# Attention with mixed heads and a mixture of experts: two pairs of heads of scores in one step, products with v and a third of the rows in the next, on the same banks

## The chip, the cores and the metric

One core of a Trainium2 chip runs the whole program. The metric is the device time of one execution in microseconds (us). PE is TensorE, DVE VectorE, ACT ScalarE, POOL GpSimd, and SP the engine whose queue issues most transfers.

## What is computed

```python
scores = (1/8) * q @ k.T                       # 8 batches, 12 heads, 448 x 448, 64 columns a head
scores = einsum('bhij,hg->bgij', scores, w_pre)
attn = softmax(scores)                         # over j
attn = einsum('bhij,hg->bgij', attn, w_post)
x = (attn @ v) as 3584 rows of 768
logits = x @ w_gate; e = argmax(logits); p = softmax(logits)[e]
out = p * (relu(x @ w1[e]) @ w2[e])            # one of 8 experts for each row
```

## The kernel before

**Attention.** Each batch of 448 queries is cut into four tiles T of 120, 120, 120 and 88 queries, 32 tiles in all. Heads go in pairs (6 pairs c or p). For a tile the scores of one pair (`qk`, L231: six matmuls, with q and k each split in a rounded high part and a remainder) go to the two banks `bank_s`, and ACT copies them to the tile's buffer `SI` (`evict_s`, L243). SP then issues transfers that turn a *block* of up to 20 queries so that (query, head) lies along the partitions (`relayout`, L251, tiles `sb`, four buffers). A tile of 120 queries has 6 blocks, one of 88 has 5, the last of them a single half. So a batch has 23 blocks and the program 184, and there is one *step* u for each.

In step u one block goes through each stage: `mix` (L258, PE, scores mixed over heads by w_pre, into `bank_m`), `maxima` (L271, DVE), `powers` (L278, ACT, exponentials and their sums). In step u+1 follow `recip` (L287, DVE) and `weigh` (L294, POOL), in step u+2 `post` (L303, PE, mixing by w_post, into `bank_p`) and `evict_p` (L319, DVE, into the tile's `PT`). `bank_m` and `bank_p` have one buffer each, so a step's mix follows the exponentials of the step before.

Beside that the steps carry work of other tiles. Before the change each step has `qk` and `evict_s` of one pair of the next tile, 8 to 3 steps ahead of its first block (QLEAD, L482), and `av` (L341, eight matmuls of one pair's PT with v) of the tile before, into `bank_a`, half of the pairs in each of its two banks. After three pairs `evict_x` (L350, DVE) copies the products out, `rows` (L361, PE, three matmuls with the identity and w_gate beside it) turns them into rows, `evict_r` (L367, ACT) copies the rows out and `logits` (L374, DVE) adds up the gate's part. When a tile's rows are complete, `store_x` (L382, SP) writes them to memory, `choose`, `rank`, `place`, `token` (L391 to L446) pick each row's expert and count, and `scatter` (L448, POOL) writes the row's number and weight into a table.

**The order** is written by hand. `at(u, stage, ...)` puts a call in step u (L485), ORDER (L549) gives the order of the stages within a step, and the loop at L578 emits them so; each engine keeps that order. `load_v` of the next batch (L147: 1152 KB and twice 192 KB) stands in a batch's step 9, after that step's `relayout` and `store_x`. For the first tile of a batch the scores of pair 0 come last in their step (stage "qk2").

**The end of attention.** The first expert's six tiles of w1 are loaded and split (`load_w`, L470: a transfer of 512 KB, a copy on ACT, a subtraction on DVE) one in each of the last steps from L586 on, load and split in the same step. All six `av` of the last tile stand at the end of its last step.

**The experts.** L592 on is the same in both kernels: each expert's rows are gathered through the table, transposed and multiplied, PE without a pause. The first gather needs the table and the rows of the last tile.

Of the kernel before, what the change touches and what calls it, by code (L numbers as in the profile page):

```python
# [42 lines left out]
def attn_moe_kernel(ctx, tc, qT, kT, v, w_pre, w_post, w_gate, w1, w2, out):  # L43
# [46 lines left out]
    bank_s = ps_s.tile([P, 2, 512], F32, name="bs")  # L90
    bank_a = ps_s.tile([P, 2, 512], F32, name="ba")
# [139 lines left out]
    def qk(T, c, bank):  # L231
        b, it, ni = geom[T][:3]
        if c == 0:
            SI[T] = si_p.tile([IT, H, S], F32, name="si")
        qh, ql = QQ[T]
        kh, kl = KK[b, c]
        for n, (qx, kx) in enumerate(((qh, kh), (qh, kl), (ql, kh))):
            for r in range(2):
                hs = slice(r * D, (r + 1) * D)
                nc.tensor.matmul(out=bank[:ni, r, :S], lhsT=qx[hs, c, :ni],  # L240
                                 rhs=kx[hs, :], start=(n == 0), stop=(n == 2))

    def evict_s(T, c, bank, copy):  # L243
        ni = geom[T][2]
        copy(out=SI[T][:ni, 2 * c:2 * c + 2, :], in_=bank[:ni, :, :S])  # L245
# [92 lines left out]
    def acc(g):  # L338
        return bank_a[:, g, :3 * IT].rearrange("p (c i) -> p c i", i=IT)

    def av(T, p):  # L341
        b, it, ni = geom[T][:3]
        for c in range(NJ):
            for r in range(2):
                h = 2 * p + r
                nc.tensor.matmul(out=acc(p // 3)[r * D:(r + 1) * D, p % 3, :ni],  # L346
                                 lhsT=VV[b][:, c, h * D:(h + 1) * D],
                                 rhs=PT[T][:, c, h, :ni], start=(c == 0), stop=(c == NJ - 1))

    def evict_x(T, g):  # L350
        ni = geom[T][2]
        if g == 0:
            XT[T] = x_p.tile([P, NPAIR, IT], F32, name="xt")
        nc.vector.tensor_copy(out=XT[T][:, 3 * g:3 * g + 3, :ni], in_=acc(g)[:, :, :ni])  # L354
# [3 lines left out]
    def rows_bank(part):  # L358
        return bank_a[:, part, :3 * XG].rearrange("p (c x) -> p c x", x=XG)

    def rows(T, part):  # L361
        ni = geom[T][2]
        for c in range(3):
            nc.tensor.matmul(out=rows_bank(part)[:ni, c, :], lhsT=XT[T][:, part * 3 + c, :ni],
                             rhs=xg[:, part * 3 + c, :], start=True, stop=True)

    def evict_r(T, part):  # L367
        ni = geom[T][2]
        if part == 0:
            XR[T] = x_p.tile([IT, NPAIR, P], F32, name="xr", bufs=1)  # L370
        nc.scalar.copy(out=XR[T][:ni, part * 3:part * 3 + 3, :],
                       in_=rows_bank(part)[:ni, :, :P])

    def logits(T, part):  # L374
        ni = geom[T][2]
        if part == 0:
            LG[T] = sm_p.tile([IT, 2, NE], F32, name="lg")
        nc.vector.reduce_sum(out=LG[T][:ni, part, :],
                             in_=rows_bank(part)[:ni, :, P:XG].rearrange("p c e -> p e c"),
                             axis=AX.X)  # L380
# [8 lines left out]
    RK = slice(496, 496 + NE), slice(496 + NE, 512)  # L389

    def choose(T):  # L391
        b, it, ni = geom[T][:3]
        lg2 = LG.pop(T)
        lg = sm_p.tile([IT, NE], F32, name="lgs")
        nc.vector.tensor_add(out=lg[:ni], in0=lg2[:ni, 0, :], in1=lg2[:ni, 1, :])
# [12 lines left out]

    def rank(T):
        ni = geom[T][2]  # L410
        ohb = DD[T][2]
        for lhs, m, cols in ((tri[:ni, :ni], ni, RK[0]), (ones[:ni, :], P, RK[1])):
            nc.tensor.matmul(out=bank_a[:m, 1, cols], lhsT=lhs, rhs=ohb[:ni], start=True, stop=True)
# [8 lines left out]
    def place(T):  # L422
# [3 lines left out]
        nc.vector.tensor_tensor(out=pos[:ni], in0=bank_a[:ni, 1, RK[0]], in1=state["base"][:ni],  # L426
# [3 lines left out]
        nc.vector.tensor_tensor(out=nbase, in0=bank_a[:, 1, RK[1]], in1=state["base"], op=ALU.add)  # L430
# [42 lines left out]


# [13 lines left out]
    vec, act = nc.vector.tensor_copy, nc.scalar.copy  # L488
    for u, (T, s) in enumerate(blocks):
        at(max(u - RLEAD, -1), "relayout", relayout, T, s)  # L490
        at(u, "mix", mix, T, s)
        at(u, "max", maxima, T, s)
        at(u, "exp", powers, T, s)
        at(u + 1, "recip", recip, T, s)
        at(u + 1, "weigh", weigh, T, s)
        at(u + PL, "post", post, T, s)
        at(u + PL, "evict_p", evict_p, T, s)
    for T in range(NTILE):
        b, it, ni = geom[T][:3]
        u0, n = ustart[T], len(geom[T][3])  # L500
        if T > 1:
            at(u0 - 12, "load", load_q, T)
            for part in range(2):
                at(u0 - 10 + part, "split", split_q, T, part)
        if T:
            for c in range(NPAIR):
                u = u0 - QLEAD + c
                if u < 0:
                    continue
                late = c == 0 and it == 0  # L510
                at(u, "qk2" if late else "qk", qk, T, c, bank_s)
                at(u, "evict_s2" if late else "evict_s", evict_s, T, c, bank_s, act)
        if it == 0 and b + 1 < B:
            U = ustart[T + 4]
            at(u0 + 9, "load", load_v, b + 1)
            for c, (ul, us) in enumerate(((15, 12), (14, 11), (10, 8), (9, 7), (7, 6), (6, 5))):
                at(U - ul, "load", load_k, b + 1, c)
                at(U - us, "split", split_k, b + 1, c)
        w = u0 + n + PL
        if T + 1 == NTILE:  # L520
            seq = [w - 1] * NPAIR
        elif T + 2 == NTILE:
            seq = [w + p // 2 for p in range(NPAIR)]
        else:
            m = len(geom[T + 1][3])
            seq = [w + max(p - (NPAIR - m), 0) for p in range(NPAIR)]
        last = T + 1 == NTILE
        for p in range(NPAIR):
            at(seq[p], "av_last" if last else "av", av, T, p)
        for g in range(2):  # L530
            u = seq[3 * g + 2] + 1
            at(u, "vec", evict_x, T, g)
            at(u, "rows", rows, T, g)
            at(u, "evict_r", evict_r, T, g)
            at(u + 1, "vec", logits, T, g)
        u = seq[5] + 2
        at(u, "store", store_x, T)
        near = T + 2 >= NTILE
        u += not near
        at(u, "vec", choose, T)  # L540
        at(u, "rank", rank, T)
        at(u, "gate", gate, T)
        u += 1
        at(u, "vec", place, T)
        u += not near
        at(u, "vec", token, T)
        at(u, "scatter", scatter, T)

    ORDER = ("relayout", "store", "load", "mix", "recip", "vec", "weigh", "scatter", "max", "exp",  # L549
             "post", "qk", "rank", "av", "rows", "gate", "evict_p", "av_last", "evict_s", "qk2",  # L550
             "evict_r", "split", "evict_s2")
# [3 lines left out]
    banks = (bank_s, bank_a)  # L555
    split_q(0, 0)
    pend = []
    for c in range(NPAIR):
# [4 lines left out]
        qk(0, c, banks[c % 2])  # L563
        pend.append((0, c, banks[c % 2], vec if c % 2 else act))
        if c:
            evict_s(*pend.pop(0))
    evict_s(*pend.pop(0))
    for part in range(2):
        split_q(1, part)
    load_v(0)  # L570
    for what in steps.pop((-1, "relayout")):
        what[0](*what[1:])
    for c in range(2):
        qk(1, c, banks[c % 2])
        evict_s(1, c, banks[c % 2], vec if c % 2 else act)

    last_u = max(u for u, _ in steps)
    for u in range(0, last_u + 1):  # L578
# [3 lines left out]
        if u == ustart[NTILE - 1] - 2:  # L582
# [3 lines left out]
        if u > ustart[NTILE - 1] - 3 and u - ustart[NTILE - 1] + 3 <= NK1:  # L586
            load_w(0, w1, u - ustart[NTILE - 1] + 2, FF, "a")
# [267 lines left out]
```

## Time and profile before

| | |
|---|---|
| median of 3 runs | 1358.95 us (1357.21 to 1364.66) |
| profiled execution | 1356.08 us, its span 1354.4 us, mean granted clock 0.965 |
| busy | PE 1269.2, DVE 774.4, ACT 673.1, POOL 371.4 us |
| attention | from the first mix at 23.1 us to the last table write at 797.66 us |
| experts | first transposes at 810.49 us, to the end |

A busy PE is not PE at its peak, since matmuls overlap and their ends are modelled. What a piece of work takes is therefore read from where the next piece starts. PEclk is the granted clock, 1.0 for the 2.4 GHz level and 0.5 for the 1.2 GHz level.

### The profile page before, as it was taken

How to read it: one execution, taken by the hardware profiler on the slowest of the kernel's cores; microseconds unless marked ns; L12 is line 12 of the kernel's file. 1: busy time of each engine (PE TensorE's matmuls, PEld its weight loads, DVE VectorE, ACT ScalarE, POOL GpSimd, SP SyncE). 2: the span in 40 equal slices, each digit the busy share in tenths (PEclk: the TensorE clock that was granted, in tenths of full speed). 3: DMA queues.
4: the chain of work that ended last, by engine and by line, in shares of the span. 5: the costliest groups of instructions: out<-in, count | busy, mean ns of one | idle time of the engine just before them, and what ended most of it. 6: DMA issues, size and time to landing. Idle time of an engine off the chain costs nothing. (4 is left out here: it accounts for less than half of the span.)

```text
span 1354.4 us, 45076 instructions
## 1 busy us (share of the span) xinstructions
PE 1269.2 (94%) x18960; PEld 1014.6 (75%) x18960; DVE 774.4 (57%) x2027; ACT 673.1 (50%) x1436; POOL 371.4 (27%) x605
## 2 busy tenths in 40 slices
PE   6999999999899999999998739999999999999995
PEld 3677677677676676776775539989898989989985
DVE  4777677778678677777776634433434343444220
ACT  4776576667666665766675313332333333333220
POOL 3353343443433433433432121202020202020000
PEclk8999999999899899999999878999999999999998
DMA  6644745655546547456534233625252626354210
GB/s 204 197 145 154 191 144 168 185 169 162 164 149 188 163 140 202 137 176 191 162 133 163 89 114 109 202 95 184 82 193 72 202 74 207 131 165 151 83 37 31
DMA packets 115295, 200.08 MB, mean 148 GB/s; under 512 B 40003, under 2 KB 89171, under 8 KB 115077
## 3 DMA queue, kind: packets, MB, share of 16 engines
q1 hardware_dynamic: 107968, 173.08, 40.8%
q0 software_dynamic: 6064, 23.86, 5.1%
q8 instruction: 161, 2.64, 0.9%
q14 instruction: 58, 0.47, 0.1%
q10 hardware_dynamic: 1044, 0.04, 0.0%
HBM read 97.59 MB, written 23.06 MB: 89 GB/s over the span
## 5 line engine op out<-in xcount | busy, mean ns | idle before, releaser
L282 ACT ACTIVATE et<-bm,st 124x448 f32<-124x448 f32 x360 | 225.3, 631 | 214.9 <-DVE st L274 212.0
L274 DVE TENSOR_REDUCE st<-bm 124x1 f32<-124x448 f32 x360 | 207.8, 617 | 95.5 <-PE bm L268 89.5
L315 PEld LDWEIGHTS bp<-wp,et 60*64 60x64 f32 (+1 forms) x10080 | 193.3, 137 | 86.8 <-issue 77.6
L333 DVE COPY pt<-bp 128x480 f32<-128x480 f32 x352 | 213.2, 647 | 3.1 <-PE bp L315 2.7
L268 PE MATMUL bm<-sb,Wquad 60*60 60x448 f32 (+3 forms) x1408 | 191.1, 582 | 17.6 <-DMA sb<-si 16.2
L299 POOL TENSOR_SCALAR wp<-Wpost,st 124x60 f32<-124x60 f32 x360 | 151.6, 435 | 193.0 <-DVE st L292 82.6
L346 PE MATMUL ba<-pt,vt 128*64 128x120 f32 (+1 forms) x3072 | 191.2, 270 | 10.0 <-DVE xt L354 7.5
L346 PEld LDWEIGHTS ba<-pt,vt 128*64 128x64 f32 x3072 | 152.7, 140 | 57.1 <-DVE st L274 28.6
L315 PE MATMUL bp<-wp,et 60*64 60x60 f32 (+1 forms) x10080 | 193.6, 221 | 2.0 <-issue 2.0
L245 ACT COPY si<-bs 120x896 f32<-120x896 f32 (+1 forms) x188 | 169.1, 900 | 12.7 <-PE bs L240 12.6
L675 PE MATMUL pm_h<-xh,ah 128*128 128x512 f32 (+1 forms) x384 | 146.4, 381 | 1.9 <-ACTq L734 1.5
L705 POOL DMA_INDIRECT out<-y,ti x30 | 30.0, 999 | 424.9 <-ACT y L703 415.8
L675 PE MATMUL pm_h<-xl,ah 128*128 128x512 f32 (+1 forms) x384 | 146.5, 381 | 0.0
L675 PE MATMUL pm_h<-xh,al 128*128 128x512 f32 (+1 forms) x384 | 144.8, 377 | 0.0
L679 DVE SCALAR_TENSOR_TENSOR hl<-pm_h,hh 128x512 fp32r<-128x512 f32 (+1 forms) x64 | 42.1, 658 | 158.9 <-ACT hh L678 158.9
L696 PE MATMUL pm_y<-bh,hh 128*128 128x384 f32 x480 | 124.7, 341 | 0.0
L678 ACT ACTIVATE hh<-pm_h 128x512 fp32r<-128x512 f32 (+1 forms) x64 | 36.6, 572 | 174.9 <-PE pm_h L675 174.9
L696 PE MATMUL pm_y<-bl,hh 128*128 128x384 f32 x480 | 122.3, 336 | 0.0
L696 PE MATMUL pm_y<-bh,hl 128*128 128x384 f32 x480 | 122.3, 336 | 0.0
L143 POOL TENSOR_TENSOR ql<-qr,qh 128x360 fp32r<-128x360 f32 (+1 forms) x78 | 70.1, 910 | 164.7 <-ACT qh L142 154.9
L240 PE MATMUL bs<-kh,qh 64*120 64x448 f32 (+1 forms) x376 | 87.7, 463 | 11.0 <-ACT kh L116 7.3
L703 ACT ACTIVATE y<-pm_y,tb 128x384 f32<-128x384 f32 x30 | 17.5, 582 | 146.2 <-PE pm_y L696 87.9
(115 smaller groups left out, 1783.0 us busy)
## 6 DMA issues: line engine op xcount, KB each, us to landing
sb<-si SPq DMA_DIRECT2D x344, 210.0 KB
wraw<-in_w SPq DMA_DIRECT2D x48, 512.0 KB
wraw<-in_w SPq DMA_DIRECT2D x64, 384.0 KB
kr<-in_kT SPq DMA_DIRECT2D x42, 224.0 KB
vt<-in_v SPq DMA_DIRECT2D x8, 1152.0 KB
qr<-in_qT SPq DMA_DIRECT2D x48, 180.0 KB
XD<-xr SPq DMA_DIRECT2D x24, 360.0 KB
vt<-in_v SPq DMA_DIRECT2D x16, 192.0 KB
```

Source lines behind the costliest of these rows:

```text
L143: (nc.vector if T == 0 else nc.gpsimd).tensor_sub(out=lo, in0=src, in1=hi.bitcast(F32))
L240: nc.tensor.matmul(out=bank[:ni, r, :S], lhsT=qx[hs, c, :ni], rhs=kx[hs, :], start=(n == 0), stop=(n == 2))
L245: copy(out=SI[T][:ni, 2 * c:2 * c + 2, :], in_=bank[:ni, :, :S])
L268: nc.tensor.matmul(out=bank_m[r][CUT[c], :S], lhsT=Wquad[CUT[r], CUT[c]], rhs=sb[CUT[r], c, :], start=True, stop=True)
L274: nc.vector.reduce_max(out=st[:R1, 0, c:c + 1], in_=bank_m[c][:R1, :S], axis=AX.X, negate=True)
L282: nc.scalar.activation(out=et[:R1, c, :], in_=bank_m[c][:R1, :S], func=AF.Exp, bias=st[:R1, 0, c:c + 1], scale=1.0, accum_out=st[:R1, 1, c ...
L299: nc.gpsimd.tensor_scalar(out=wp[:R1, c, :], in0=Wpost[:R1], scalar1=st[:R1, 2, c:c + 1], scalar2=None, op0=ALU.mult)
L315: nc.tensor.matmul(out=bank_p[r][col * JC:(col + 1) * JC, at_:at_ + W], lhsT=et[CUT[r], n, kg * JC:(kg + 1) * JC], rhs=wp[CUT[r], n, :], s ...
L333: nc.vector.tensor_copy(out=flat[:, :, i0 + r * IB:i0 + (r + 1) * IB] .rearrange("p x (n k) -> p x n k", k=IQ), in_=bank_p[r][:, :2 * NJ * ...
L346: nc.tensor.matmul(out=acc(p // 3)[r * D:(r + 1) * D, p % 3, :ni], lhsT=VV[b][:, c, h * D:(h + 1) * D], rhs=PT[T][:, c, h, :ni], start=(c ...
L675: nc.tensor.matmul(out=ph[:, :n], lhsT=wx[:, fs], rhs=xx[:, kt, :n], start=(m == 0), stop=(m == 3 * NK1 - 1))
L696: nc.tensor.matmul(out=py[g][:, :384], lhsT=hx[:, kt, ts], rhs=wx[:, g * 384:(g + 1) * 384], start=(n == 0), stop=(n == 3 * NK2 - 1))
```

## The change

The four banks of `bank_s` and `bank_a` become two tiles `bank_s[0]` and `bank_s[1]` of two banks each. Scores of an even pair go to the first, of an odd pair to the second. In a step with scores (qsteps: a tile's steps 0, 2 and 4) `qk` and `evict_s` of two pairs stand, last in the step. In the steps between (vsteps: 1, 3 and 5, or 4 where the tile has five) `av` of two pairs stands, into `bank_s[0]`, with `rows` of two earlier pairs into `bank_s[1]`. Products leave at the start of the next step (`evict_x`), or in the same step, ahead of its scores, where a step has both ("vec_now", once in a batch). So a third of a tile's products is copied, turned and evicted at a time. `logits` is gone: `evict_r` copies the gate's columns too, and `choose` adds all six up at once. `store_x` writes runs of 128 numbers instead of whole rows of 768. Loads and splits of q and k stand at other steps. At the end, w1 is fetched from step NU-3 on and split two steps after (`fetch_w`, `split_w`), and the last tile's `av`, `evict_x` and `rows` are interleaved.

```diff
-    bank_s = ps_s.tile([P, 2, 512], F32, name="bs")
-    bank_a = ps_s.tile([P, 2, 512], F32, name="ba")
+    bank_s = [ps_s.tile([P, 2, 512], F32, name=f"bs{n}") for n in range(2)]
...
-    def av(T, p):
+    HOME = {g: bank_s[0][:, 0, :] for g in range(3)}
+    def av(T, g):
...
+        for p in range(2):
+            for c in range(NJ):
+                for r in range(2):
+                    h = 4 * g + 2 * p + r
+                    nc.tensor.matmul(out=HOME[g][r * D:(r + 1) * D, p * IT:p * IT + ni],
+                                     lhsT=VV[b][:, c, h * D:(h + 1) * D],
+                                     rhs=PT[T][:, c, h, :ni], start=(c == 0), stop=(c == NJ - 1))
...
-        nc.sync.dma_start(out=XD[t0:t0 + ni, :],
-                          in_=XR.pop(T)[:ni].rearrange("p c x -> p (c x)"))
+        nc.sync.dma_start(out=XD[t0:t0 + ni, :].rearrange("t (c x) -> t c x", x=P),
+                          in_=XR[T][:ni, :, :P])
...
+        for g, (dt, k) in enumerate(((2, 4), (1, 0), (1, 2))):
+            if T + dt < NTILE:
+                qsteps[T + dt, g] = u0 + k
...
+            for g, (dt, k) in enumerate(((1, 3), (1, n - 1), (2, 1))):
+                if T >= dt:
+                    vsteps[T - dt, g] = u0 + k
...
+    for kt in range(NK1):
+        at(NU - 3 + kt, "fetch", fetch_w, kt)
+        at(NU - 1 + kt, "split_w", split_w, kt)
...
+            for g in range(3):
+                av(T, g)
+                evict_x(T, g)
+                if g:
+                    rows(T, g - 1, bank_m[g - 1])
+                    evict_r(T, g - 1)
+            rows(T, 2, bank_s[1][:, 1, :])
+            evict_r(T, 2)
```

PE in two steps in the middle of the program. bm is `bank_m`, bp `bank_p`, bs the score banks (bs_101 and bs_102 the two tiles after the change), ba `bank_a`; the rows of `post` between mix and scores are left out. Before, each step is alike:

```order
L268 MATMUL bm_104<-sb_149,Wquad 60x448
...
L240 MATMUL bs<-kh,qh 120x448 x2
L240 MATMUL bs<-kl,qh 120x448 x2
L240 MATMUL bs<-kh,ql 120x448 x2
L346 MATMUL ba<-pt,vt 64x120 x8
```

With the change, a step with scores and the step after it:

```order
L239 MATMUL bs_101<-kh,qh 120x448 x2
L239 MATMUL bs_101<-kl,qh 120x448 x2
L239 MATMUL bs_101<-kh,ql 120x448 x2
L239 MATMUL bs_102<-kh,qh 120x448 x2
L239 MATMUL bs_102<-kl,qh 120x448 x2
L239 MATMUL bs_102<-kh,ql 120x448 x2
L267 MATMUL bm_103<-sb_149,Wquad 64x448
...
L346 MATMUL bs_101<-pt,vt 64x120 x16
L363 MATMUL bs_102<-xg,xt 120x136 x2
```

Two pairs of scores now stand together, and 16 products with two matmuls of rows in the next step; before it was one pair and 8 products in each step, with three matmuls of rows in two steps of a tile.

SP around the load of the next batch's v (vt), in the middle of the program. kr is k, qr q, XD the rows in memory. Before:

```order
L255 DMA sb_151<-si 120x1x448 x2
L385 DMA XD<-xr 88x768
L150 DMA vt<-in_v 128x3x768
L154 DMA vt<-in_v 64x768 x2
L109 DMA kr<-in_kT 128x448
L255 DMA sb_148<-si 120x1x448 x2
```

With the change:

```order
L254 DMA sb_151<-si 120x1x448 x2
L149 DMA vt<-in_v 128x3x768
L153 DMA vt<-in_v 64x768 x2
L108 DMA kr<-in_kT 128x448
L254 DMA sb_148<-si 120x1x448 x2
L254 DMA sb_149<-si 120x1x448 x2
L375 DMA XD<-xr 528x1x128
```

The store of the rows, which stood ahead of vt, now stands behind the two blocks after it.

## Rows read from the trace of the kernel before

**Rows 1.** The page: busy time, share of the span and instructions of PE and the other engines.

```profile
PE 1269.2 (94%) x18960; PEld 1014.6 (75%) x18960; DVE 774.4 (57%) x2027; ACT 673.1 (50%) x1436; POOL 371.4 (27%) x605
```

**Rows 2.** The table by stretches: stretch and length in us, then busy us and count of PE, PEld, DVE, ACT and POOL, the granted clock, the share of the DMA engines and GB/s. First 600 us of attention, then its last steps.

```profile
100.00:700.00 600.00, 583.72 (x13002) 416.41 (x12994) 440.57 (x1373) 401.98 (x937) 246.58 (x415) 0.98 0.55 166
733.87:797.66 63.79, 41.36 (x828) 33.21 (x826) 36.69 (x129) 19.25 (x47) 9.37 (x19) 0.85 0.31 97
```

**Rows 3.** The timeline of an ordinary step, PE and its weight loads (PEld): start us, us, engine, line, operation, tiles, shapes, count.

```profile
331.83 0.98 PE L268 MATMUL bm<-sb,Wquad 64*64 64x448 f32 x8
332.63 0.99 PE L315 MATMUL bp<-wp,et 64*64 64x60 f32 x56
333.55 0.47 PE L240 MATMUL bs<-kh,qh 64*120 64x448 f32 x2
333.65 0.18 PEld L240 LDWEIGHTS bs<-kl,qh 64*120 64x120 f32 x2
333.86 0.36 PE L240 MATMUL bs<-kl,qh 64*120 64x448 f32 x2
334.06 0.37 PE L240 MATMUL bs<-kh,ql 64*120 64x448 f32 x2
334.36 1.04 PE L346 MATMUL ba<-pt,vt 128*64 128x120 f32 x16
335.32 0.98 PE L268 MATMUL bm<-sb,Wquad 64*64 64x448 f32 x8
```

**Rows 4.** The timeline of PE where two pairs of products stand together, followed by three matmuls of rows and the next mix.

```profile
102.17 1.86 PE L346 MATMUL ba<-pt,vt 128*64 128x120 f32 x32
103.97 0.95 PE L364 MATMUL ba<-xg,xt 128*120 128x136 f32 x6
104.85 0.98 PE L268 MATMUL bm<-sb,Wquad 64*64 64x448 f32 x8
```

**Rows 5.** The timeline of PE in the first steps, which have no products yet: the first and the last of four mixes, three steps apart.

```profile
37.79 1.21 PE L268 MATMUL bm<-sb,Wquad 64*64 64x448 f32 x6
46.64 1.11 PE L268 MATMUL bm<-sb,Wquad 64*64 64x448 f32 x8
```

**Rows 6.** Groups by line from 100 to 700 us, ACT's exponentials and its evictions of scores: busy us, mean ns, then idle us before and what ended it.

```profile
L282 ACT ACTIVATE et<-bm,st 124x448 f32<-124x448 f32 x289 | 180.9, 631 | 164.3 <-DVE st L274 161.3 <-issue 3.0
L245 ACT COPY si<-bs 120x896 f32<-120x896 f32 (+1 forms) x155 | 139.4, 900 | 4.4 <-PE bs L240 4.4
```

**Rows 7.** The timeline of PE, mixes alone: steps 11, 12 and 13 of the fourth batch, then three ordinary steps of the same make (the first with rows, the second without).

```profile
338.95 0.98 PE L268 MATMUL bm<-sb,Wquad 64*64 64x448 f32 x8
346.02 2.21 PE L268 MATMUL bm<-sb,Wquad 64*64 64x448 f32 x5 [2.66 <-DMA sb<-si]
352.83 0.98 PE L268 MATMUL bm<-sb,Wquad 64*64 64x448 f32 x8
...
369.38 0.98 PE L268 MATMUL bm<-sb,Wquad 64*64 64x448 f32 x8
373.76 0.98 PE L268 MATMUL bm<-sb,Wquad 64*64 64x448 f32 x8
377.26 0.98 PE L268 MATMUL bm<-sb,Wquad 64*64 64x448 f32 x8
```

**Rows 8.** The timeline of SP's queue around that place (issues, with the time they took to issue).

```profile
332.44 0.31 SPq L385 DMA_DIRECT2D XD<-xr  x1
332.84 0.42 SPq L150 DMA_DIRECT2D vt<-in_v  x1
336.94 3.50 SPq L255 DMA_DIRECT2D sb<-si  x4
```

**Rows 9.** The table by stretches, columns as in the second group: one microsecond at that place.

```profile
336.00:337.00 1.00, 1.00 (x60) 0.85 (x52) 0.93 (x6) 0.37 (x2) 0.64 (x1) 1.00 1.02 366
```

**Rows 10.** The timeline of PE: two mixes of the first batch, its steps 10 and 12, then mixes of single halves, one in each batch's last step: those of the first, the third, the fourth and the seventh batch.

```profile
56.83 0.98 PE L268 MATMUL bm<-sb,Wquad 64*64 64x448 f32 x8
...
68.54 0.98 PE L268 MATMUL bm<-sb,Wquad 64*64 64x448 f32 x8
...
108.35 1.02 PE L262 MATMUL bm<-sb,Wpre 124*124 124x448 f32 x2
...
294.05 1.01 PE L262 MATMUL bm<-sb,Wpre 124*124 124x448 f32 x2
...
389.44 1.02 PE L262 MATMUL bm<-sb,Wpre 124*124 124x448 f32 x2
...
669.94 1.02 PE L262 MATMUL bm<-sb,Wpre 124*124 124x448 f32 x2
```

**Rows 11.** The timeline of the last steps: PE's mix of step 176 (of 0 to 183), ACT's first copy of w1, PE's products after it, PE's last mix (step 183), the last tile's products, and the last write to the table.

```profile
730.41 0.98 PE L268 MATMUL bm<-sb,Wquad 64*64 64x448 f32 x8
...
741.59 1.04 ACT L467 CAST ah<-wraw 128x1024 fp32r<-128x1024 f32 x1 [4.21 <-DMA wraw<-in_w]
...
745.31 1.87 PE L346 MATMUL ba<-pt,vt 128*64 128x120 f32 x16 [6.38 <-DVE xt L354]
...
769.38 1.02 PE L262 MATMUL bm<-sb,Wpre 124*124 124x448 f32 x2
...
784.65 5.51 PE L346 MATMUL ba<-pt,vt 128*64 128x88 f32 x96 [0.39 <-DVE pt L327]
...
797.66 0.99 POOL L451 DMA_INDIRECT TB<-tg,di  x1 [5.09 <-DVE sidx L649]
```

More of the change, by code (lines that the diff above doesn't have):

```diff
@@ L350, in evict_x @@
     def evict_x(T, g):
         ni = geom[T][2]
-        if g == 0:
-            XT[T] = x_p.tile([P, NPAIR, IT], F32, name="xt")
-        nc.vector.tensor_copy(out=XT[T][:, 3 * g:3 * g + 3, :ni], in_=acc(g)[:, :, :ni])
-    XR, LG, DD = {}, {}, {}
[L358 to L380, printed above, removed]
+        XT[T, g] = x_p.tile([P, 2, IT], F32, name="xt", bufs=3)
@@ new lines, in evict_x, with rows @@
+        nc.vector.tensor_copy(out=XT[T, g][:, :, :ni],
+                              in_=HOME[g][:, :2 * IT].rearrange("p (c i) -> p c i", i=IT)[:, :, :ni])
+    XR, LG, DD = {}, {}, {}
+    def rows(T, g, bank):
+        ni = geom[T][2]
+        xt = XT.pop((T, g))
+        SHEET[T, g] = bank[:, :2 * XG].rearrange("p (c x) -> p c x", x=XG)
+        for c in range(2):
+            nc.tensor.matmul(out=SHEET[T, g][:ni, c, :], lhsT=xt[:, c, :ni],
+                             rhs=xg[:, 2 * g + c, :], start=True, stop=True)
@@ L382, in store_x, with evict_r @@
+    def evict_r(T, g):
+        ni = geom[T][2]
+        if g == 0:
+            XR[T] = x_p.tile([IT, NPAIR, XG], F32, name="xr", bufs=2)
+        nc.scalar.copy(out=XR[T][:ni, 2 * g:2 * g + 2, :], in_=SHEET.pop((T, g))[:ni])
     def store_x(T):
@@ L472, in load_w, with fetch_w, split_w @@
         fill_w(e, w, kt, width, nm)
+    RAW = {}
+    def fetch_w(kt):
+        take_w(0, kt, FF, "a")
+        RAW[kt] = wpool["raw"].tile([P, FF], F32, name="wraw")
+        nc.sync.dma_start(out=RAW[kt], in_=w1[0, kt * P:(kt + 1) * P, :])
+    def split_w(kt):
+        hi, lo = W["a", 0, kt]
+        raw = RAW.pop(kt)
+        nc.scalar.copy(out=hi, in_=raw)
+        nc.vector.tensor_sub(out=lo, in0=raw, in1=hi.bitcast(F32))
     ustart, blocks = [], []
@@ L500, in attn_moe_kernel @@
         u0, n = ustart[T], len(geom[T][3])
+        last = T + 1 == NTILE
         if T > 1:
-            at(u0 - 12, "load", load_q, T)
+            up = ustart[T - 2]
+            at(up, "load", load_q, T)
             for part in range(2):
[L504 to L512, printed above, removed]
+                at(up + 1 + 2 * part, "split", split_q, T, part)
+        for g in range(3):
+            for c in (2 * g, 2 * g + 1):
+                if (T, g) in qsteps:
+                    at(qsteps[T, g], "qk", qk, T, c)
+                    at(qsteps[T, g], "evict_s", evict_s, T, c)
         if it == 0 and b + 1 < B:
@@ L527, in attn_moe_kernel @@
[L527 to L540, printed above, removed]
+            for c in range(NPAIR):
+                at(U - 18 + 2 * c, "load", load_k, b + 1, c)
+                at(U - 15 + 2 * c, "early", split_k, b + 1, c)
@@ new lines, in attn_moe_kernel @@
+        if last:
+            continue
+        for g in range(3):
+            u = vsteps[T, g]
+            at(u, "av", av, T, g)
+            both = u in hasq
+            at(u if both else u + 1, "vec_now" if both else "vec", evict_x, T, g)
+            u = free(u + 1)
+            bank = bank_s[1][:, used.get(u, 0), :]
+            used[u] = used.get(u, 0) + 1
+            at(u, "rows", rows, T, g, bank)
+            at(u + 1, "evict_r", evict_r, T, g)
+        at(u + 2, "store", store_x, T)
@@ L541, in attn_moe_kernel @@
+        at(u + 2, "vec", choose, T)
+        u = free(u + 3) if T + 3 < NTILE else u + 2
         at(u, "rank", rank, T)
         at(u, "gate", gate, T)
[L543 to L551, printed above, removed]
+        at(u + 1, "vec", place, T)
@@ L552, in attn_moe_kernel @@
+        at(u + 2, "vec", token, T)
+        at(u + 2, "scatter", scatter, T)
+    for kt in range(NK1):
+        at(NU - 3 + kt, "fetch", fetch_w, kt)
+        at(NU - 1 + kt, "split_w", split_w, kt)
+    ORDER = ("relayout", "store", "load", "fetch", "mix", "recip", "vec", "weigh", "scatter",
+             "evict_r", "early", "max", "exp", "post", "rank", "av", "rows", "gate", "evict_p",
+             "vec_now", "qk", "evict_s", "split", "split_w")
     manual = ctx.enter_context(ExitStack())
@@ L562, in attn_moe_kernel @@
             load_q(1)
-        qk(0, c, banks[c % 2])
-        pend.append((0, c, banks[c % 2], vec if c % 2 else act))
+        qk(0, c)
         if c:
[L566 to L569, printed above, removed]
+            evict_s(0, c - 1, act if c % 2 else vec)
+    evict_s(0, NPAIR - 1, vec)
     load_v(0)
@@ L572, in attn_moe_kernel @@
         what[0](*what[1:])
+    for part in range(2):
+        split_q(1, part)
     for c in range(2):
[L574 to L578, printed above, removed]
+        qk(1, c)
+        evict_s(1, c, act if c % 2 else vec)
+    for u in range(max(u for u, _ in steps) + 1):
         for stage in ORDER:
```

74 lines of the change are left out of this document (39 added, 35 removed).

## The prediction

> **What bounds the kernel now.** I read the busy times first: PE is busy 94% of the span, no other engine over 57% [rows 1]. The table by stretches then parts the program. From 100 to 700 us PE is busy 583.7 of 600 us at a granted clock of 0.98, and DVE and ACT have a quarter to a third of their time free; in the last 64 us of attention PE is busy 41 us at a clock of 0.85 [rows 2]. The experts after that are the same code, so only attention can change.
>
> Next the timeline of one step [rows 3], taken from start to start: mix 0.80, post 0.92, one pair of scores 0.81, one pair of products 0.96, in all 3.49 us with no pause. Three matmuls of rows, in two steps of a tile, add 0.88 [rows 4]. So an ordinary step ends with PE. But PE follows a ring too: mix, maximum, exponential, next mix. In the first steps, where PE has no products, three steps take 8.85 us, 2.95 each [rows 5], and that is the least a step can take.
>
> Last I looked for steps that are longer than this, and found two places.
>
> First, a stall in each batch. Mix 12 of the fourth batch starts 7.07 us after mix 11, and mix 13 another 6.81 after that, 13.88 together; a like pair of steps takes 7.88 [rows 7]. The loss is 6.00. PE waited for sb, and the mix itself then took 2.21, more than twice the usual 0.98. SP's queue shows why: the store of rows XD went out at 332.44, and only behind it could v of the next batch go (332.84), with sb for the stalled mix behind that, at 336.94 [rows 8]. v is 1.5 MB, and the engines moved it at 366 GB/s with a share of 1.02, all they have [rows 9].
>
> Second, the end. From mix 176 to mix 183 there are 38.97 us, and 28.28 more to the last write [rows 11]. ACT waits 4.21 us for the first tile of w1, which was asked for in the same step; DVE waits behind ACT with its copy of the products, and PE 6.38 us behind DVE [rows 11].
>
> **The change, part by part.**
>
> *The stall of each batch.* The seventh batch's last mix is 561.59 us after the first's, six batches. The fourth takes 95.39, without its 6.00 it takes 89.39; six of these are 536.34. So the six stalls cost 25.2. In the first batch, steps 10 and 11 take 11.71 against 7.88, another 3.8 [rows 7, 10]. Sum: 29.0. With the change, XD is no longer ahead of v. v's buffer comes free with the products of the old batch in step 7, so v starts about the end of step 7, a step earlier than now. sb for mix 12 waits for the scores' copies of step 8, done about 1.9 us into step 9 (two copies of 0.90 behind the exponentials [rows 6]). From the end of step 7 to there lie a step with scores and 1.9 us, over 5 us, in which v and one tile of k (1.76 MB at 366 GB/s, 4.8 us) are through. From there to mix 12 are the rest of step 9 and steps 10 and 11, about 9.6 us. Now sb went out 6.4 us ahead of its mix's place (338.95 plus 4.38, less 336.94) and came 2.7 late, 9.1 in all with v ahead of it [rows 7, 8]. So even an unchanged transfer would just make it. Bounds 0 and 29; I take all 29.
>
> *Packing on PE.* Two adjacent pairs of products take 1.80 [rows 4] where two single ones take 1.92 [rows 3]: 0.12 less for each two steps. Rows come in three groups of two a tile instead of two of three: a group of two costs between 0.59 (two thirds of 0.88) and 0.70 (the whole start-up of about 0.1, the first score matmul's 0.31 over the next one's 0.20 [rows 3]); I take 0.64, so 0.05 lost. Two adjacent pairs of scores are not in the trace. The second costs between 0.81, as the first, and 0.60, three matmuls at 0.20 apart [rows 3]. I take the middle, 0.71: 0.10 less. The row for the middle: the weights of kl are loaded at 333.65 while the matmul before runs on the same rows from 333.55 to 334.02 [rows 3], so loads can hide, but the last of three took 0.30 to the next kind of work.
>
> Here a rule speaks against the change. The Trainium skill, "TensorE: Matmul & The Clock Gate", section "The mechanism", says that a weight load overlaps running matmuls only when it goes to another group of rows. By it adjacent pairs would save nothing. The trace differs: the load just named lies wholly inside a matmul of its own rows.
>
> So a step with scores takes 0.80 + 0.92 + 0.81 + 0.71 = 3.24, above the ring's 2.95, and one with products 0.80 + 0.92 + 1.80 + 0.64 = 4.16; 0.17 less than two steps before, for some 90 such twos: 15 us. Against that ACT and DVE get fuller. In 600 us, 147 steps, DVE is busy 440.57 and ACT 401.98 [rows 2], so 6.0 and 5.5 us in two steps of 7.40. Both evictions now come at the end of a step; the second runs 1.9 us into the next, about when its exponentials can begin, after its mix and the first maximum. Some steps will wait a tenth or two. I take 7 off and keep 8. Bounds: 24 gained, 18 lost (0.2 a pair).
>
> Once in a batch a step has both kinds, and its scores wait for the products' copy, about 0.5 us. Before, the late scores of pair 0 waited likewise; nothing.
>
> *The end.* No scores are left after step 175. Steps 176 to 182 are then 4.16, 2.95 (rows alone, so the ring), 3.51, 2.95, 3.51, 4.16 and 4.16: 25.4 against 38.97 [rows 11], 13.6 less. It holds if w1 lands before its split; it is asked for behind the last sb and split two steps later, over 7 us, and now the first lands 4.2 us late when split at once. From mix 183 to the last write I keep 28.3. Three splits more stand ahead of the last tile's choice; but the products, 5.51 us in one piece [rows 11], are interleaved with their copies and rows. Bounds for the end: 7 to 18; I take 13.
>
> *At nothing:* runs of 512 bytes in the store (nobody waits for it but the experts, and the last store has the table's way to hide behind), the lost `logits` and the regrouped copies on DVE, the earlier q and k loads (SP has room when nothing blocks it).
>
> Sum: 29 + 8 + 13 = 50. Against the profiled 1356.08 that is 1306; against the median, 2.9 higher, 1309. I say **1308**.
>
> **Rivals.**
> 1. *sb is late all the same*, behind v or behind tiles of k that wait for POOL to free their buffer. For it: the transfers run full for microseconds [rows 9]. Against: the 3 us of slack above. Then 29 are not gained: 1337. Chance 0.11.
> 2. *Adjacent pairs save nothing*, the weight loads standing between matmuls: 8 not gained, 1316. The rule named above is this one. Chance 0.13; the weight load in [rows 3] speaks against it.
> 3. *The end does not shorten*, since w1 waits for the memory it takes over or DVE's splits crowd the last tile: 1321. Chance 0.11.
> 4. *Slower.* ACT has two evictions of 0.90 and two exponentials of 0.63 [rows 6], with the reading of sums some 3.4 us, in a step of 3.24. If the spill delays the next exponentials, and through the one `bank_m` the next mix, each two steps lengthen. It decides where they lose 0.55 us more than they gain by packing (50 over 90). At 0.8 us a pair, 72 in all, the time is 1308 + 8 + 72 = 1388. Against: a step with products has 4.16 us, and 1.9 plus two exponentials end at 3.5. Chance 0.05.
>
> **How the numbers follow.** The forecast has 0.60: 1292 to 1324 by the bounds of packing and end. Rival 1 widens the range to 1340; below I end at 1288. That leaves out rival 4 and what lies beyond the bounds, under 0.2. A measurement tells about 0.5%, 7 us, from no change. Faster takes the forecast and rivals 1 to 3 but for a small part where two of them meet: 0.91. Same 0.04, slower 0.05.
>
> **What would show it.** Right: no mix waits for sb at step 12 and batches are under 88 us apart; steps alternate near 3.2 and 4.2; mix 183 is 25 to 28 us after mix 176; no ACT wait for w1. Packing is wrong if two steps sum to 7.55 or more with PE unbroken; rival 4 is right if mixes wait for ACT's exponentials in most steps with products. A stall at another step of the batch would make the prediction wrong, and so would a new wait of scores for copies.

## The result, and the profile after

The changed kernel takes 1300.93 us (median of 4 runs, 1297.11 to 1308.47) beside 1360.24 us (1357.21 to 1364.66): a ratio of 0.957, with an interval of 0.952 to 0.962. The forecast was 1308. The two profiled executions differ by 54.6 us (spans 1354.4 and 1299.8), and the marks of [rows 10] and [rows 11] part this difference:

| stretch | before | after | difference |
|---|---|---|---|
| start to first mix | 23.13 | 22.38 | -0.8 |
| first mix to the first batch's last mix | 85.22 | 82.60 | -2.6 |
| that to the seventh batch's last mix (six batches) | 561.59 | 522.09 | -39.5 |
| that to mix 176 | 60.47 | 60.20 | -0.3 |
| mix 176 to mix 183 | 38.97 | 27.14 | -11.8 |
| mix 183 to the last table write | 28.28 | 28.89 | +0.6 |
| last table write to the end | 556.74 | 556.50 | -0.2 |

The table by stretches, as [rows 2], for the middle and the last steps:

```profile
100.00:680.00 580.00, 575.59 (x13460) 448.67 (x13460) 469.44 (x1394) 420.90 (x998) 252.72 (x429) 1.00 0.57 177
687.27:753.00 65.73, 42.56 (x928) 34.52 (x926) 42.43 (x151) 22.42 (x57) 15.59 (x25) 0.83 0.42 120
```

In the middle PE is now busy 575.6 of 580 us, at a granted clock of 1.00 where it was 0.98: with the stalls gone, the drops to 0.5 that followed four of the six are gone too. The second stretch reaches 9.7 us past the last table write; from mix 176 to that write the clock was 0.88, and 0.86 before the change.

Two steps of the middle, PE alone, as [rows 3] and [rows 4]: the scores of one step, then a whole step with products.

```profile
171.42 0.47 PE L239 MATMUL bs<-kh,qh 64*120 64x448 f32 x2
171.73 0.37 PE L239 MATMUL bs<-kl,qh 64*120 64x448 f32 x2
171.93 0.36 PE L239 MATMUL bs<-kh,ql 64*120 64x448 f32 x2
172.13 0.36 PE L239 MATMUL bs<-kh,qh 64*120 64x448 f32 x2
172.33 0.37 PE L239 MATMUL bs<-kl,qh 64*120 64x448 f32 x2
172.53 0.36 PE L239 MATMUL bs<-kh,ql 64*120 64x448 f32 x2
172.82 1.16 PE L267 MATMUL bm<-sb,Wquad 64*64 64x448 f32 x8
173.63 1.17 PE L314 MATMUL bp<-wp,et 64*64 64x60 f32 x56
174.73 1.86 PE L346 MATMUL bs<-pt,vt 128*64 128x120 f32 x32
176.52 0.72 PE L363 MATMUL bs<-xg,xt 128*120 128x136 f32 x4
177.17 0.98 PE L267 MATMUL bm<-sb,Wquad 64*64 64x448 f32 x8
```

Read starts against starts. The first pair of scores takes 0.71 to the start of the second, and the second one's matmuls start 0.20 apart like those within a pair. Both take 1.40, where two single pairs took 1.62 [rows 3]. The products take 1.79 and the rows 0.65. But `post` takes 1.10 to the products, where [rows 3] has 0.92, and this mix lasts 1.16 instead of 0.98. ACT's two exponentials of the step before show why:

```profile
171.63 0.64 ACT L281 ACTIVATE et<-bm,st 124x448 f32<-124x448 f32 x1 [0.97 <-DVE st L273]
172.25 0.63 ACT L281 ACTIVATE et<-bm,st 124x448 f32<-124x448 f32 x1
```

The second ends at 172.88, when the mix has begun (172.82) in the bank that the first left free. The mix's second half, into the other bank, starts at 173.02 and is 0.2 us late; the first half does not wait.

SP's queue around the load of v of the fourth batch (as [rows 8]), and PE's mixes 11, 12 and 13 of it (as [rows 7]):

```profile
313.45 0.39 SPq L149 DMA_DIRECT2D vt<-in_v  x1
...
318.77 3.52 SPq L254 DMA_DIRECT2D sb<-si  x4
322.38 0.82 SPq L375 DMA_DIRECT2D XD<-xr  x1
```

```profile
324.43 1.09 PE L267 MATMUL bm<-sb,Wquad 64*64 64x448 f32 x8
328.70 0.98 PE L267 MATMUL bm<-sb,Wquad 64*64 64x448 f32 x8
331.81 1.08 PE L267 MATMUL bm<-sb,Wquad 64*64 64x448 f32 x8
```

The transfer of v goes out 15.3 us ahead of mix 12 (before, 13.2 us ahead of a mix that was itself late), the store behind it, and mix 12 waits for nothing.

The mixes of single halves, as [rows 10]: 

```profile
104.98 0.92 PE L261 MATMUL bm<-sb,Wpre 124*124 124x448 f32 x2
...
279.16 0.92 PE L261 MATMUL bm<-sb,Wpre 124*124 124x448 f32 x2
...
366.06 0.92 PE L261 MATMUL bm<-sb,Wpre 124*124 124x448 f32 x2
...
627.07 0.92 PE L261 MATMUL bm<-sb,Wpre 124*124 124x448 f32 x2
```

The fourth batch takes 86.90 us (95.39 before), and 87.0 is the mean of six.

The end, as [rows 11], PE and POOL: mix 176, the last tile's products, the last ranking, the last table write.

```profile
687.27 1.08 PE L267 MATMUL bm<-sb,Wquad 64*64 64x448 f32 x8
...
723.79 2.62 PE L346 MATMUL bs<-pt,vt 128*64 128x88 f32 x32 [1.35 <-DVE pt L326]
726.85 2.62 PE L346 MATMUL bs<-pt,vt 128*64 128x88 f32 x32 [0.44 <-DVE xt L353]
...
730.30 1.43 PE L346 MATMUL bs<-pt,vt 128*64 128x88 f32 x32
...
740.25 0.17 PE L404 MATMUL bs<-ohb,tri 88*88 88x8 bf16 x1 [6.80 <-DVE sc L396]
...
743.30 0.99 POOL L442 DMA_INDIRECT TB<-tg,di  x1 [3.29 <-DVE cum L689]
```

No wait for w1 is left, but PE stands 6.80 us before the last ranking, since DVE's choice of the last tile comes after three splits. Two of the three groups of products take 2.62, one 1.43, the same work: the granted clock was 0.50 in the first two and 1.00 in the third.

### The profile page after: what moved, and what is told of

Same layout as the page of the kernel before. It is cut to its first block, busy times and chain, and to the rows that moved or that the text cites. A ratio compares the mean times of both kernels' runs of the same rounds, so it can differ in the third digit from the quotient of the medians.

```text
span 1299.8 us, 45032 instructions
## 1 busy us (share of the span) xinstructions
PE 1234.3 (95%) x18960; PEld 1032.0 (79%) x18960; DVE 787.9 (61%) x1995; ACT 679.0 (52%) x1468; POOL 371.8 (29%) x605
## 5 line engine op out<-in xcount | busy, mean ns | idle before, releaser
L273 DVE TENSOR_REDUCE st<-bm 124x1 f32<-124x448 f32 x360 | 208.1, 619 | 90.3 <-PE bm L267 85.7
L314 PEld LDWEIGHTS bp<-wp,et 60*64 60x64 f32 (+1 forms) x10080 | 199.8, 135 | 71.2 <-issue 48.7
L267 PE MATMUL bm<-sb,Wquad 60*60 60x448 f32 (+3 forms) x1408 | 188.3, 566 | 5.9 <-ACT et L281 4.5
L346 PE MATMUL bs<-pt,vt 128*64 128x120 f32 (+1 forms) x3072 | 173.5, 265 | 2.5 <-DVE pt L326 1.4
L244 ACT COPY si<-bs 120x896 f32<-120x896 f32 (+1 forms) x188 | 160.8, 910 | 26.4 <-PE bs L239 25.4
L346 PEld LDWEIGHTS bs<-pt,vt 128*64 128x64 f32 x3072 | 151.5, 138 | 9.1 <-issue 2.0
L239 PE MATMUL bs<-kh,qh 64*120 64x448 f32 (+1 forms) x384 | 82.0, 423 | 12.2 <-ACT kh L115 7.3
```

What stands on the lines that cost most here:

```text
L239: nc.tensor.matmul(out=bank_s[c % 2][:ni, r, :S], lhsT=qx[hs, c, :ni], rhs=kx[hs, :], start=(n == 0), stop=(n == 2))
L244: copy(out=SI[T][:ni, 2 * c:2 * c + 2, :], in_=bank_s[c % 2][:ni, :, :S])
L267: nc.tensor.matmul(out=bank_m[r][CUT[c], :S], lhsT=Wquad[CUT[r], CUT[c]], rhs=sb[CUT[r], c, :], start=True, stop=True)
L273: nc.vector.reduce_max(out=st[:R1, 0, c:c + 1], in_=bank_m[c][:R1, :S], axis=AX.X, negate=True)
L314: nc.tensor.matmul(out=bank_p[r][col * JC:(col + 1) * JC, at_:at_ + W], lhsT=et[CUT[r], n, kg * JC:(kg + 1) * JC], rhs=wp[CUT[r], n, :], s ...
L346: nc.tensor.matmul(out=HOME[g][r * D:(r + 1) * D, p * IT:p * IT + ni], lhsT=VV[b][:, c, h * D:(h + 1) * D], rhs=PT[T][:, c, h, :ni], start ...
```

## The experiments

**1. The loads ahead of the store, in the kernel before.**

```diff
-    ORDER = ("relayout", "store", "load", "mix", ...
+    ORDER = ("relayout", "load", "store", "mix", ...
```

> The kernel before, with the loads of v, k and q put ahead of the store of the rows XD in each step, and nothing else changed. Theory (v of the next batch waits in SP's queue behind the store, and sb of mix 12 behind v): no mix waits for a transfer in steps 11 to 14 of a batch, batches are 89.4 us apart instead of 93.6, and the time falls by 25 to 29 us, to about 1333. Rival (the store has little to do with it; what the changed kernel does earlier with scores, k and q removes the stall): less than 10 us gained, and a mix of steps 11 to 14 still waits for sb.

1337.74 us, a ratio of 0.985 (0.982 to 0.989): 20 us gained. No mix behind the first waits for a transfer any more, so the stall is what the theory says. But batches are 90.9 us apart and not 89.4: PE loses time at another place, which experiment 2 shows.

**2. The load of v alone ahead of it.**

```diff
-            at(u0 + 9, "load", load_v, b + 1)
+            at(u0 + 9, "load_v", load_v, b + 1)
...
-    ORDER = ("relayout", "store", "load", "mix", ...
+    ORDER = ("relayout", "load_v", "store", "load", "mix", ...
```

> The kernel before, with the load of v alone put ahead of the store; k and q stay behind it. Moving all loads gained about 20 us where the stalls had held 26.7 in six batches and some in the first: 10 of that came back, 1.0 a batch of it in step 6, where PE stood twice, 0.16 and 0.60 us, with no wait that the profile shows. Theory (k and q, moved too, are what PE's new pauses come from): the pauses in step 6 are gone, batches are 89 to 89.5 us apart, and 25 to 29 us are gained. Rival (the pauses come whenever the stall is gone, whoever was moved): step 6 stays 1 us longer, batches are 90.3 to 91.6 apart, and some 20 us are gained.

1334.69 us, a ratio of 0.980 (0.977 to 0.983): 26 us between the medians, 27 by the ratio. PE, step 6 of the fourth batch; "issue" marks idle time for which the profile shows no wait:

```profile
313.32 0.98 PE L268 MATMUL bm<-sb,Wquad 64*64 64x448 f32 x8
314.12 0.74 PE L315 MATMUL bp<-wp,et 64*64 64x60 f32 x36
315.01 0.35 PE L315 MATMUL bp<-wp,et 60*64 60x60 f32 x4 [0.15 <-issue]
315.99 0.54 PE L315 MATMUL bp<-wp,et 64*64 64x60 f32 x16 [0.63 <-issue]
...
334.34 0.98 PE L268 MATMUL bm<-sb,Wquad 64*64 64x448 f32 x8
338.69 0.98 PE L268 MATMUL bm<-sb,Wquad 64*64 64x448 f32 x8
342.16 0.98 PE L268 MATMUL bm<-sb,Wquad 64*64 64x448 f32 x8
```

The last three rows are mixes 11 to 13: 7.82 us, the length of an undisturbed pair, where [rows 7] has 13.88. Counted so, the six stalls of the profiled run before held 26.6 us (six pairs of steps, 73.5 us in all, less 6 times 7.82). But `post` of step 6 pauses, once or twice, in every batch behind the first, and the step takes 4.6 to 4.7 us instead of 3.6 to 3.8. So the pauses come whoever was moved, and the rival wins on the place and on the batches (90.3 to 92.2). Its reason, that they come because the stall is gone, does not hold: the kernel of experiment 3 has them in the same step, with its stalls in place. The time lies nearer to the theory's. Six batches take 544.51 us, 17.1 less than in [rows 10]; 5.8 of the missing 9.5 are step 6. The trace of the kernel before has no such pause in the six batches and one of 2.01 us in the first; the changed kernel has 1.00 us there, and from 100 to 680 us none. What PE lacks in them, what brings them, and why these two kernels are free of them, no run here tells.

**3. w1 split two steps after its fetch, in the kernel before.**

```diff
...
-            load_w(0, w1, u - ustart[NTILE - 1] + 2, FF, "a")
+        kt = u - ustart[NTILE - 1] + 2
+        if 2 <= kt < NK1 + 2:
+            split_w(kt - 2)
+        if 0 <= kt < NK1:
+            fetch_w(kt)
...
```

> The kernel before, with each tile of w1 split two steps after its fetch instead of in the same step; the fetches stay where they are, and so do the products, copies and rows of the last tiles. Theory (ACT's wait for w1, with DVE and PE behind it, makes most of the long end): no ACT wait for w1 stands ahead of a copy that PE needs, mixes 176 to 183 take 28 to 31 us instead of 39.0, and the time falls by 8 to 11 us. Rival (the changed kernel's end is short because its last products and rows are regrouped): less than 4 us gained.

1356.31 us, a ratio of 0.998 (0.995 to 1.001): 3 us by the medians, and not to be told from none. Mix 176 stands at 737.41 and mix 183 at 766.12, 28.7 us as the theory has it, against 38.97. Some of the gain was given back behind: from mix 183 to the last write 32.85 us instead of 28.28. A late split on DVE now stands ahead of a copy of products that PE's rows wait for; and 1.2 of the 4.6 are the last products, 6.66 instead of 5.51, at a granted clock of 0.56 instead of 0.69. The split, and PE's rows:

```profile
776.17 1.23 DVE L485 TENSOR_TENSOR al<-wraw,ah 128x1024 fp32r<-128x1024 f32 x1 [4.40 <-ACT ah L484]
778.98 0.93 PE L364 MATMUL ba<-xg,xt 128*120 128x136 f32 x6 [3.38 <-DVE xt L354]
```

From mix 176 to the last write the end is 5.7 us shorter. The rest of that trace was longer: its six batches took 569.5 us, 7.9 more, with the same order as before. The stalls, counted as in experiment 2, are 27.5 us of it, only 0.9 more; 5.8 are step 6, which takes 4.65 to 4.73 and has the pauses of experiments 1 and 2. The fourth batch:

```profile
323.17 0.55 PE L315 MATMUL bp<-wp,et 64*64 64x60 f32 x16 [0.62 <-issue]
```

So these pauses do not need the stall to be gone. The theory is right on the place and wrong on the gain, of which pauses elsewhere took a part in this trace.

**4. Edits 1 and 3 together.**

> The two edits on the kernel before together, loads ahead of the store and w1 split two steps after its fetch. Theory (stall and end are separate places): the gains add, 34 to 40 us, a time of 1319 to 1326; what the changed kernel has beyond this, some 18 to 25 us, is packing on PE and the regrouped end. Rival (both are one shortage of transfers or of SP): under 30 us.

1331.61 us, a ratio of 0.982 (0.978 to 0.987): 24 us (27 between the medians), under the rival's bound. Its reason does not show: the six batches fell by 16.7 us, as in experiment 1 (16.3), and the stretch from mix 176 to the last write by 6.3, as in experiment 3 (5.7). The two gains do add, but each is smaller than expected, for the reasons of experiments 1 to 3. The changed kernel is 30 us below this one. By the traces 22.8 of that lie in the six batches and 7 from the seventh batch's last mix to the last write.

**5. Products in pairs of heads, scores left alone, in the kernel before.**

```diff
-            seq = [w + max(p - (NPAIR - m), 0) for p in range(NPAIR)]
+            seq = [w, w, w + 2, w + 2, w + 4, w + 4]
...
-            at(u, "rows", rows, T, g)
-            at(u, "evict_r", evict_r, T, g)
+            late = T + 2 < NTILE
+            at(u + late, "rows", rows, T, g)
+            at(u + late, "evict_r", evict_r, T, g)
...
```

> The kernel before, with the products of two pairs of heads in every second step and most of the rows with them, while the scores stay at one pair in each step. Theory (a step cannot be shorter than the ring of mix, maximum and exponential, 2.95 us, so products may only be bunched if scores fill the steps between): the steps without products are 2.95 to 3.1 us though their work on PE is 2.53, the steps with products 4.3 to 5.2; two steps lengthen by 0.30 to 0.45 and the time by 27 to 40 us. Rival (PE alone counts, and adjacent pairs save 0.12 for each two steps): 11 us faster.

1403.74 us, a ratio of 1.034 (1.030 to 1.038): 45 us slower. PE in two steps, the mix of the first, then from the second mix on:

```profile
296.38 0.98 PE L268 MATMUL bm<-sb,Wquad 64*64 64x448 f32 x8
...
299.03 1.21 PE L268 MATMUL bm<-sb,Wquad 64*64 64x448 f32 x6
299.83 0.39 PE L315 MATMUL bp<-wp,et 64*64 64x60 f32 x8
300.07 0.54 PE L268 MATMUL bm<-sb,Wquad 60*64 60x448 f32 x2
300.44 0.97 PE L315 MATMUL bp<-wp,et 60*64 60x60 f32 x48
301.35 0.47 PE L240 MATMUL bs<-kh,qh 64*120 64x448 f32 x2
...
304.83 0.98 PE L268 MATMUL bm<-sb,Wquad 64*64 64x448 f32 x8
```

The pair takes 8.45 us where PE's work would be 7.74 (twice 3.49 and 0.88, less 0.12). The light step is only 2.65 long; the ring shows one step on, where the second half of the mix waits for the second exponential: its last two matmuls start 1.04 after the first (0.44 in the step before), with matmuls of `post` in the gap, and 2.32 lie from the mix to the scores instead of 1.72. So direction and mechanism are the theory's, while its place and its size (0.59 more than the 7.86 of before, not 0.30 to 0.45) were not. The stalls behind v grew as well, to waits of 3.2 to 4.6 us for sb; they are about 9 of the 43 us by which the six batches grew. By this, bunched products pay only where the scores fill the other steps.

**6. The two pairs of scores apart, in the changed kernel.**

```diff
-                    at(qsteps[T, g], "qk", qk, T, c)
+                    uq = qsteps[T, g]
+                    at(uq, "qk_even" if c % 2 == 0 and uq not in vs else "qk", qk, T, c)
...
-             "evict_r", "early", "max", "exp", "post", "rank", "av", "rows", "gate", "evict_p",
+             "evict_r", "early", "max", "exp", "qk_even", "post", "rank", "av", "rows", "gate", "evict_p",
```

> The changed kernel, with the two pairs of scores of a step apart on PE: the even pair right after the mix, the odd pair after post as now. ACT's copies stay at the end of the step, and the one step of a batch that has both kinds stays as it is. Theory (the second of two adjacent pairs costs 0.60 us instead of 0.81, since only the first has a start-up): a step with scores lengthens by about 0.2 us, 3.12 to 3.3, some 83 times: 14 to 18 us slower. Rival (a weight load overlaps only matmuls on other rows, so that adjacent pairs save nothing, and steps with scores are short for another reason): within 4 us of the changed kernel.

1327.66 us (1322.31 to 1330.37): 27 us slower than the changed kernel. One step, PE; its mix starts at 202.35:

```profile
203.26 0.47 PE L239 MATMUL bs<-kh,qh 64*120 64x448 f32 x2
...
204.06 1.04 PE L314 MATMUL bp<-wp,et 64*64 64x60 f32 x56
205.03 0.47 PE L239 MATMUL bs<-kh,qh 64*120 64x448 f32 x2
...
205.83 0.98 PE L267 MATMUL bm<-sb,Wquad 64*64 64x448 f32 x8
```

The step is 3.48 long instead of 3.12, with no wait: mix 0.91, scores 0.80, `post` 0.97, scores 0.80. So not only the second pair grows, by 0.20; the mix ahead of scores takes 0.10 more and `post` behind them 0.05. Each change of kind on PE has its price, and adjacency saves three. The first four of the six batches take 89.2 us here and 87.0 in the changed kernel, 2.2 more. Eleven times 0.36 would be 4.0: a part comes back in the steps with products, whose mixes are hardly late any more (0.4 us a batch instead of 1.3 to 1.8). The theory's direction stands, and 2.2 a batch, some 17 us in all by estimate, lies in its range; its sum of the price does not, and the rival is out. The time grew by some 10 us more than that. Of the 28.7 us between the two spans, 7 lie behind the last table write, in the same code, with one pause of PE marked "issue" of 3.6, and two more such pauses, 1.5 and 1.8, lie in the sixth and seventh batch.

**7 to 9. Three places of the changed kernel, one by one.** The splits of w1:

```diff
-        at(NU - 1 + kt, "split_w", split_w, kt)
+        if kt < 2:
+            at(NU - 1 + kt, "split_w", split_w, kt)
...
     scatter(T)
+    for kt in range(2, NK1):
+        split_w(kt)
```

> The changed kernel, with the splits of the last four of the six tiles of w1 put behind the last tile's write to the table. Theory (they stand on ACT and DVE ahead of the last tile's copies and choice, and PE waits 6.8 us for that choice): from the last mix to the last table write 19 to 24 us instead of 28.9, and 5 to 9 us faster. Rival (the chain of products, copies, rows, choice and table sets the length by itself, at the lower clock): less than 3 us.

The order of scores in the step that has both kinds:

```diff
+    vs = set(vsteps.values())
...
-            for c in (2 * g, 2 * g + 1):
+            odd_first = qsteps.get((T, g)) in vs
+            for c in (2 * g + 1, 2 * g) if odd_first else (2 * g, 2 * g + 1):
```

> The changed kernel, with the odd pair's scores ahead of the even pair's in the one step of a batch that has products and scores; their bank does not wait for the copy of the products. Theory (PE stands still for that copy, about 0.5 us, as I put at nothing in the prediction): that step falls from 5.6 to 5.1 us, and the time by 3 to 4 us. Rival (the next step's exponentials come later by as much, since ACT's copies set it): no change.

The copies of the first steps:

```diff
-                    at(qsteps[T, g], "evict_s", evict_s, T, c)
+                    at(qsteps[T, g], "evict_s", evict_s, T, c,
+                       vec if c % 2 and qsteps[T, g] < 9 else act)
```

> The changed kernel, with the copies of the odd pairs' scores on DVE instead of ACT in the first nine steps, where PE has no products. Theory (there ACT's two copies spill into the next step and delay its exponentials, as in rival 4, and the mixes wait 0.8 to 1.6 us for them): the first nine steps take 30 to 31 us instead of 33.5, and 2.5 to 3.5 us are gained. Rival (the waits come from the relayout of the first blocks or from k and q): no change.

Medians of 1299.95, 1299.24 and 1302.20 us (ratios to before 0.956, 0.954 and 0.958): none can be told from the changed kernel's 1300.93 by time, whose runs spread over 11 us. The traces do tell. The splits: PE's wait for the last choice is 2.45 instead of 6.80, and mix 183 to the last write takes 23.44 us instead of 28.89, as in the theory:

```profile
735.18 0.17 PE L404 MATMUL bs<-ohb,tri 88*88 88x8 bf16 x1 [2.45 <-DVE sc L396]
```

The order of scores: the step with both kinds, in the changed kernel and then with the odd pair first (its mix at 278.93, the next at 283.96):

```profile
280.98 1.86 PE L346 MATMUL bs<-pt,vt 128*64 128x120 f32 x32
283.35 0.46 PE L239 MATMUL bs<-kh,qh 64*120 64x448 f32 x2 [0.51 <-DVE st L289]
```

```profile
280.75 1.86 PE L346 MATMUL bs<-pt,vt 128*64 128x120 f32 x32
282.54 0.46 PE L239 MATMUL bs<-kh,qh 64*120 64x448 f32 x2
```

The step takes 5.03 instead of 5.59, and six batches 518.59 instead of 522.09, 3.5 less. The early copies: the first nine steps take 30.96 us instead of 33.54, but mixes still wait 1.1 us for ACT's exponentials every second step, and the granted clock of that stretch was 1.00 in this trace and 0.90 in the changed kernel's, so that the edit is not shown to be the cause. The changed kernel's own rows speak against its theory:

```profile
42.32 1.72 ACT L244 COPY si<-bs 120x896 f32<-120x896 f32 x2
45.08 0.63 ACT L281 ACTIVATE et<-bm,st 124x448 f32<-124x448 f32 x1 [1.04 <-DVE st L273]
```

```profile
45.86 1.21 PE L267 MATMUL bm<-sb,Wquad 64*64 64x448 f32 x6 [1.25 <-ACT et L281]
```

ACT had been done with its copies for 1.04 us when the exponential began; it waited for DVE's maximum. The mixes wait for the ring, not for the copies.

**10. All three.**

> The changed kernel with three edits together: the last four splits of w1 behind the last table write, the odd pair's scores first in the step that has both kinds, and the odd pairs' copies on DVE in the first nine steps. Theory (the three places are separate stretches of one chain, so what their traces showed adds: 5.4 us in the last stretch, 3.5 over six batches and some 0.6 for each other one, 3.7 in the first batch): from the first mix to the last table write 720.9 less 12 to 13, and a median of 1286 to 1291 us. Rival (the clock or another engine gives it back, since the single edits' medians moved by 2 us at most): a median of 1296 to 1302.

1294.18 us (1290.97 to 1301.91), a ratio of 0.952 (0.948 to 0.956): the lowest median of all, 7 below the changed kernel's, between the two cases, with an interval that still meets the changed kernel's. From the first mix to the last write it is 712.35 us instead of 720.92, 8.6 less: 6.2 in the last stretch, 2.8 in the six batches, 0.5 in the batch after, and 0.9 lost in the first batch, where PE's pauses marked "issue" are 2.13 and 0.31 us, beside 1.00 in the changed kernel.

## Why the prediction was right, step by step

**The stall: 29, right as a size, wrong in a part.** The six stalls held 26.6 us (25.2 by my count) and the changed kernel has none; experiments 1 and 2 show that the order of v and the store is the cause. v also goes out where I put it, at the end of step 7 (313.45, mix 8 at 313.96). But of the 3.8 us for the first batch, 2.01 were a pause of PE without a wait, which I did not look up. Taking the stall away alone gives 20 to 27 us: in those traces PE has the pauses of step 6, which the changed kernel has not.

**Packing: 8, too small.** The six batches fell by 39.5; less the stalls, 12.9 are left, 2.1 a batch, where I had 1.0. The second pair of scores costs 0.59 (1.40 less 0.81), about the lower bound, and not the middle, 0.71: a score step takes 3.12 and not 3.24. Experiment 6 puts a price of 2.2 us a batch on having the pairs apart, about the whole of that gain. A step with products takes 3.92 to 4.54, mostly 4.2 to 4.4 (4.16 forecast).

**The 7 for waits: about right.** In the steps with products the second half of the mix is late behind the second exponential, as in the rows of 172.82. By the trace this happens in ten to twelve mixes of a batch, mostly by 0.1 us and at most by 0.3, and makes 1.3 to 1.8 us a batch, over 8 in the six. It is the sign that I had named for rival 4, but neither its size nor its cause: ACT stood idle for 0.97 us before those exponentials, waiting for DVE's maximum, so the spilled copies did not delay them. A step with scores, 3.12, is hardly longer than the ring, and the ring runs over a little.

**Both kinds in one step: nothing, right.** The scores wait 0.51 us for the copy, in seven batches, 3.6 us in all. In the kernel before the late scores of pair 0 waited seven times too, 0.47 to 0.75 us, also 3.6 in all. Experiment 8 shows that it can be had.

**The first steps: not in the sum.** The first nine steps grew from 30.21 to 33.54 us. At full clock two of them take 3.73 and 3.04 where the kernel before has 3.08 and 2.65: a step with two pairs of scores is long, and the next, without products, ends with PE waiting 0.8 to 1.6 us for the ring. It is the loss of experiment 5 with scores in the place of products. So the first batch gained 2.6 us, and not the 3.8 and 1.0 that I had put there.

**The ring's 2.95: not the least a step can take.** It is the mean of three steps of [rows 5], in which long and short ones alternate (3.13, 2.65, 3.08). Steps 177 and 179 of the changed kernel, with rows alone, take 2.61, and each step behind them 4.11, where I had 2.95 and 3.51.

**The rule against it.** The Trainium skill, "TensorE: Matmul & The Clock Gate", section "The mechanism", says in one sentence that a weight load overlaps running matmuls only when its group of rows differs, and in another that a load to a background weight buffer is pulled ahead as well. I had named the first alone. The trace differs from its "only": the six groups of scores from 171.42 on are all on the same rows, each matmul with weights of its own, and behind the first, which takes 0.31, they start 0.20 us apart. Whether the background buffer is the way, no run here shows.

**The end: 13, measured 11.2.** Mix 176 to mix 183 fell by 11.8 (13.6 forecast), and the last stretch rose by 0.6, where I kept it. That it stayed is the sum of two things: the products are interleaved with their rows, and three splits stand ahead of the last choice. I had named these splits; experiment 7 gives their price, 5.4 us in that stretch. Experiment 3 shows that the late split alone takes 10.2 off the stretch ahead of it, in the kernel before.

So the sum of 50 against 54.6 came from the right places. Two errors of size stand behind it, packing some 5 too low, the end 2 too high; the earlier start, 0.8, and the loss in the first steps were not in it. That these partly cancel is luck.

## What to carry to other kernels

On a queue that keeps its order, a transfer that waits for a late producer holds back everything behind it; look at what stands behind a store before moving its producer. Price adjacent matmuls of a kind by the distance between starts within a run, and each change of kind by a start-up of 0.05 to 0.2 us. A wait can hide inside a row: a merged row that lasts longer than its like is worth a look at the engine that frees its bank. And before a new pause is called the price of an edit, look for it in a run without that edit: the pauses of step 6, which seemed to come from the lost stall, stood in experiment 3 beside the stall.

## What was not expected of the hardware

PE pauses for 0.15 to 3.6 us in which the profile shows no wait, at the same step of each batch but the first in a given program (step 6 in experiments 1 to 4, with the stall behind v gone or, in experiment 3, in place), and of changing length in step 9 or 10 of the first batch (2.01, 1.00 and 2.13 us in three programs, none in experiment 9). Runs of one program differ by 4 to 15 us; these pauses and the granted clock of the first and last steps are what differs most between the traces, while the stalls held 26.6 and 27.5 us in two. And in experiment 5 matmuls of `post` on the first 64 rows started (299.83) ahead of the mix's last two on the other 60 (300.07), which stand ahead of them in the program.
